# Attention with sinks and a window, then a gated feed-forward: the third group's rows loaded ahead of the output weights, its keys turned by the DMA crossbar

## The chip, the cores and the metric

The kernel runs on one core of a Trainium2 chip. A core has TensorE (PE, matrix products, with PEld for its weight loads), VectorE (DVE), ScalarE (ACT), GpSimd (POOL) and SyncE (SP), which share one SBUF, and 16 DMA engines that serve the queues of SP, ACT and POOL. The metric is the device time of one execution in microseconds. Smaller is better.

## What is computed

The first half is attention over 4 batches, 8 heads, 768 positions and a head size of 64, where a query sees the 4 first positions (the sinks) and the last 128 up to itself. The second half is a gated feed-forward block on the 3072 rows of 512 that come out of it.

```python
def _attn_ref(q, k, v, n_sink, window):
    scores = scale * np.matmul(q, k.transpose(0, 1, 3, 2))
    keep = is_sink | in_window
    scores = np.where(keep, scores, -1000000000.0)
    ...
    a = a / (np.sum(a, axis=-1, keepdims=True) + 1e-09)
    return np.matmul(a, v).astype(np.float32)

def _moe_ref(x, w_gate, w_val, w_out):
    g = x @ w_gate
    silu = g * (1.0 / (1.0 + np.exp(-g)))
    val = x @ w_val
    return (silu * val @ w_out).astype(np.float32)
```

Inputs and output are float32; the kernel computes in bf16 with float32 sums.

## The kernel before

The attention is cut into 12 groups of 256 positions, three to a batch: groups 0 to 2 are batch 0, 3 to 5 batch 1, and so on. The feed-forward is cut into eight blocks of rows (SIZES: three of 256, four of 512, one of 256). Block 3, for one, takes its rows from groups 3 and 4.

A group goes through these steps. Its rows of k and q come in (load_nat, L106: four DMAs of 128 KB on POOL's queue, which cast to bf16; tile nat) and its v (load_v, L143, or load_vm, L120). Keys and queries are turned so that the head dimension lies on partitions, into kT and qT, which hold a batch. There are two ways of turning: step_TN (L273) makes four TensorE transposes for one tensor and one half of 128 positions and has the result copied out of PSUM; xbar (L287) has SP issue a DMA transpose for each half, two to a tensor, and no engine copies anything. Then come the scores and their exponentials (step_S1, L360, step_S2, L408, step_S3, L416: products s with 52 or 18 matrix instructions, six exponentials of 128x512 on ACT, four mask products on DVE; for a group that is not the first of its batch also the sink scores pk and their exponential es, L432 and L438), the products with the values (step_PV, L469: four steps a group, tile o; for groups that are not the first of their batch the first step begins with step_sinks, L447, whose first product reads es), the division by the sum (DVE, tiles rcp and xn) and the turn of the result into xT (step_X, L523: from group 3 on a DMA transpose on SP).

A block of the feed-forward is gates (L611: for each slice the product pg, a tanh on ACT, the product pv, two operations on DVE, into ht) and then downs (L644: for 128 rows twelve products pd with the output weights wo, copied out by ACT and stored; for blocks 0 to 2 the store is issued by ACT, then by SP).

The order is written by hand. `tc.manual_schedule()` is on, so each engine runs its instructions in the order in which the program makes them. TensorE's stream is a list of units (gates and downs), and weave (L714) puts attention steps into numbered units. In the first weave (L860) units 4 to 11 are the gates of blocks 0 and 1 together, 12 to 17 the gates of block 2, and 18 to 23 the downs of blocks 0, 1 and 2, two each. Steps that are put into a downs unit are spread over its twelve products in the order in which they are listed (L645 to L656). A step that SP or DVE has to do after a product is put off until the next flush.

Three things tie the queues together. POOL, ACT and SP each work in order, so an instruction that waits holds back everything behind it on its engine. A DMA waits until the DMA that last used its completion semaphore has landed: POOL has eight of these in rotation, and SP and ACT share eight others. And nat has a single buffer from group 4 on (natp, L64), so that the load of the next group's rows waits until the crossbar has read the group before. Two small POOL instructions are only there to hold back what follows them: behind (L701) waits until the end of a block's xT has landed, turned (L705) until a group's qT has.

Ahead of the weave POOL issues, in this order (L803 to L818): gate weights, rows and values of group 2, gate weights, the four output weights (load_out, L166, 384 KB each), rows and values of group 3, then the clearing of the sinks' tile vcl, whose eight small loads SP issues, and the building of the mask.

## Time and profile before

| | us |
|---|---|
| median of three runs | 233.8 |
| the three runs | 233.5, 233.8, 235.35 |
| the profiled execution | 233.03 |
| its span in the profile | 231.2 |
| PE busy | 226.0 (98% of the span) |
| DVE busy | 151.1 (65%) |
| ACT busy | 106.3 (46%) |
| POOL busy | 84.8 (37%) |

The granted clock of TensorE is full in all 40 slices of the page. Times within the profile count from the start of the span. In a timeline a row has start, length, engine, line, operation, tile written and tile read, shape and count; a bracket at its end is the idle time of that engine just before and what ended it. A row of the chain in order of time has start, length and what ran. Queues are shown as engines with a q (SPq, ACTq); a DMA's row there is the time that its issuing took, not its transfer.

### The profile page before, as it was taken

What the parts mean: (1) busy time and instruction counts of PE and PEld (TensorE: products, weight loads), DVE (VectorE), ACT (ScalarE), POOL (GpSimd) and SP (SyncE); (2) the same over time, 40 slices, a digit from 0 to 9 for tenths busy, and PEclk for the clock granted to TensorE, in tenths of its full rate; (3) what the DMA queues carried; (4) which work ended last, traced back from release to release, by engine and by line L of the source; (5) the groups of instructions that cost most, each with busy time, mean ns of one, the idle gap of its engine ahead of it and who ended that gap; (6) DMA issues with size and microseconds to landing.
All of it is one profiled execution on the core that took longest, in us unless ns stands there. A gap on an engine that the chain in (4) does not pass through costs nothing.

```text
span 231.2 us, 5467 instructions
## 1 busy us (share of the span) xinstructions
PE 226.0 (98%) x2171; PEld 126.8 (55%) x2171; DVE 151.1 (65%) x327; ACT 106.3 (46%) x212; POOL 84.8 (37%) x123
## 2 busy tenths in 40 slices
PE   7989999999999999999999999999999999999994
PEld 3669545786556854455454454454454544487443
DVE  5898888767650797960897960697960599778000
ACT  4784496367523827323626412735512823333221
POOL 8997965960500906904526064362000000000000
PEclk9999999999999999999999999999999999999999
DMA  7999999999998998998999999989814102000132
GB/s 134 164 188 178 179 199 206 163 155 125 154 168 211 80 132 103 145 197 124 134 124 118 147 87 203 144 107 131 94 48 136 48 0 45 3 0 0 69 116 91
DMA packets 112008, 28.04 MB, mean 121 GB/s; under 512 B 99056, under 2 KB 109040, under 8 KB 111984
## 3 DMA queue, kind: packets, MB, share of 16 engines
q0 software_dynamic: 79904, 14.29, 80.7%
q1 hardware_dynamic: 30672, 11.58, 28.5%
q10 hardware_dynamic: 1408, 1.84, 2.8%
q8 instruction: 17, 0.28, 0.5%
q14 instruction: 7, 0.06, 0.1%
HBM read 29.13 MB, written 6.29 MB: 153 GB/s over the span
## 4 chain that ended last, share of the span: by engine, by line
PE 93%; DMA 4%; DVE 1%; ACTq 0%; ACT 0%; issue 0%
PE pg L564 27%; PE pv L564 27%; PE pd L657 27%; PE o L494 3%; PE s L382 3%; DMA wg<-in_moe_w_gate_dram 3%; DMA st<-in_q_dram 2%; PE o L463 1%; PE pn L279 1%; PE o L454 1%; PE pk L432 1%; PE s L326 0%; PE px L543 0%; DVE kT L755 0%; PE pt L746 0%; PE s L765 0%
## 5 line engine op out<-in xcount | busy, mean ns | idle before, releaser
L592 DVE SCALAR_TENSOR_TENSOR u<-th,pg 128x512 bf16<-128x512 f32 x72 | 49.1, 683 | 45.3 <-ACT th L584 44.9
L564 PE MATMUL pg<-xT,wg 128*128 128x512 bf16 (+1 forms) x368 | 74.2, 333 | 0.5 <-DMA wg<-in_moe_w_gate_dram 0.5
L564 PE MATMUL pv<-xT,wv 128*128 128x512 bf16 (+1 forms) x368 | 74.1, 333 | 0.0
L584 ACT ACTIVATE th<-pg 128x512 f32<-128x512 f32 x72 | 43.8, 608 | 59.4 <-PE pg L564 59.2
L657 PE MATMUL pd<-wo,ht 128*128 128x512 bf16 (+2 forms) x300 | 65.9, 370 | 0.0
L564 PEld LDWEIGHTS <-wg 128*128 128x128 bf16 x368 | 35.2, 98 | 26.5 <-DMA wg<-in_moe_w_gate_dram 0.7
L564 PEld LDWEIGHTS <-wv 128*128 128x128 bf16 x368 | 34.6, 98 | 22.8 <-issue 0.2
L607 DVE TENSOR_TENSOR ht<-u,pv 128x512 bf16<-128x512 bf16 x60 | 41.2, 686 | 4.5 <-PE pv L564 0.4
L657 PEld LDWEIGHTS <-ht 128*128 128x128 bf16 x300 | 27.6, 98 | 28.4
L662 ACT ACTIVATE ot<-pd 128x512 f32<-128x512 f32 (+1 forms) x24 | 14.3, 595 | 50.2 <-PE pd L657 50.2
L395 ACT ACTIVATE e<-s 128x512 bf16<-128x512 f32 x54 | 28.5, 614 | 5.8 <-PE s L382 5.4
L113 POOL DMA_DIRECT2D nat<-in_k_dram x20 | 17.8, 896 | 28.6 <-DMA qT<-nat 27.1
L511 DVE TENSOR_TENSOR xn<-o,rcp 128x256 bf16<-128x256 f32 x45 | 17.9, 420 | 0.7
L128 POOL DMA_DIRECT2D vm<-in_v_dram x24 | 17.8, 772 | 1.1 <-DMA va<-in_v_dram 0.8
L113 POOL DMA_DIRECT2D nat<-in_q_dram x20 | 17.8, 908 | 1.0 <-DMA wg<-in_moe_w_gate_dram 0.8
L494 PEld LDWEIGHTS <-e 128*128 128x128 bf16 x256 | 11.5, 98 | 6.0 <-issue 0.2
L404 DVE TENSOR_TENSOR e<-e,maskq 128x768 bf16<-128x768 bf16 x24 | 13.1, 552 | 1.9 <-ACT e L395 1.9
L151 POOL DMA_DIRECT2D va<-in_v_dram x12 | 10.7, 921 | 4.5 <-DMA wo<-in_moe_w_out_dram 2.5
L703 POOL CAST warmed<-xT 1x1 f32<-1x1 bf16 x3 | 0.5, 175 | 28.5 <-DMA xT<-xn 28.5
L503 DVE RECIPROCAL rcp<-o 128x4 f32<-128x4 f32 x48 | 7.1, 171 | 4.8 <-PE o L494 4.5
L664 DVE TENSOR_SCALAR ot<-pd 128x128 f32<-128x128 f32 x1 | 0.3, 292 | 14.3 <-PE pd L657 14.3
L333 ACT ACTIVATE e<-s 128x512 bf16<-128x512 f32 x16 | 8.3, 625 | 0.3 <-PE s L326 0.3
(86 smaller groups left out, 141.4 us busy)
## 6 DMA issues: line engine op xcount, KB each, us to landing
out_dram<-ot SPq DMA_DIRECT2D x17, 256.0 KB
nat<-in_k_dram POOLq DMA_DIRECT2D x20, 128.0 KB, 4.2
nat<-in_q_dram POOLq DMA_DIRECT2D x20, 128.0 KB, 5.2
va<-in_v_dram POOLq DMA_DIRECT2D x12, 128.0 KB, 5.5
wg<-in_moe_w_gate_dram POOLq DMA_DIRECT2D x6, 256.0 KB, 7.1
wv<-in_moe_w_val_dram POOLq DMA_DIRECT2D x6, 256.0 KB, 7.6
wo<-in_moe_w_out_dram POOLq DMA_DIRECT2D x4, 384.0 KB, 11.1
out_dram<-ot ACTq DMA_DIRECT2D x6, 256.0 KB
```

The costliest lines, as they stand in the source:

```text
L113: nc.gpsimd.dma_start(x[:, i, j].rearrange("p (h d) -> p h d", d=D), src[b, :, t0:t0 + P].rearrange("h p d -> p h d"))
L128: nc.gpsimd.dma_start(vms[b][p0:p1, t - 1, :, 0:D], v[b, :, t0:t0 + p1 - p0].rearrange("h p d -> p h d"))
L395: nc.scalar.activation(e_t[g][:, e0:e0 + 512], pss[g][w, i], AF.Exp, scale=scale)
L404: nc.vector.tensor_tensor(e, e, m.broadcast_to([P, 2, 384]), op=ALU.mult)
L494: nc.tensor.matmul(o, l, r, start=(c == 0 and i == 0), stop=(i == len(mms) - 1), skip_group_check=True)
L511: nc.vector.tensor_tensor(xn, po[:, :, 0:D], rcp.broadcast_to([P, 4, D]), op=ALU.mult)
L564: nc.tensor.matmul(ps[:, i * n:(i + 1) * n], ws[fi][:, c, fo * P:(fo + 1) * P], xTs[tb][:, c], start=(c == 0), stop=(c == DMC - 1))
L584: nc.scalar.activation(th, pg, AF.Tanh, scale=0.5)
L592: nc.vector.scalar_tensor_tensor(u, th, 1.0, pg, op0=ALU.add, op1=ALU.mult)
L607: nc.vector.tensor_tensor(hts[tb][:, f:f + 512 // SIZES[tb]].rearrange("p a n -> p (a n)"), u, pv, op=ALU.mult)
L657: nc.tensor.matmul(po, hts[tb][:, f, ts * P:(ts + 1) * P], wos[f // n][:, f % n, lo:hi], start=(f == 0), stop=(f == DFC - 1))
L662: nc.scalar.activation(ot, po, AF.Copy, scale=0.5)
```

## The change

The rows and values of group 3 are loaded ahead of the four output weights, and the clearing of vcl and the sinks' small loads go ahead of both. The keys of group 3 are turned by the crossbar, two DMA transposes that SP issues as soon as the rows are there. In units 14 and 15 only the queries of group 3 are still turned on TensorE: one step of four transposes in each unit, where there were two, both copied out by ACT. Group 3's fourth product with the values moves from unit 20 into unit 19; group 4's scores (step_S1) move from the end of unit 19 into unit 20, ahead of step_S2 and step_S3.

```diff
     load_gate(5)
-    for i in range(4):
-        load_out(i)
-    load_nat(3)
-    load_v(3)
     nc.gpsimd.memset(vcl, 0.0)
     nc.gpsimd.memset(vcl[:, :, D:D + 1], 1.0)
     load_sinks(vcl, 1, B)
+    load_nat(3)
+    xbar(3, (0,))
+    load_v(3)
+    for i in range(4):
+        load_out(i)
     build_maskq()
...
-        ((14, 14, 15, 15), TN(3, "aa")),
+        ((14, 15), [A(step_TN, 3, 1, j, "aa") for j in range(2)]),
         (15, [A(xbar, 4)]), (15, [A(load_nat, 5)]), (19, [A(xbar, 5, (0,))]),
         *one(17, 3), (18, [A(step_ks, 1)]), (18, [A(step_vsb, 1)]),
-        ((19, 19, 19, 20), PVs(3)), (19, [S1(4)]), (20, [L(A(step_S2, 4), A(step_S3, 4))]), (20, Xs(3)), (20, [A(xbar, 5, (1,))]),
+        ((19, 19, 19, 19), PVs(3)), (20, [S1(4), L(A(step_S2, 4), A(step_S3, 4))]), (20, Xs(3)), (20, [A(xbar, 5, (1,))]),
```

## The prediction

> **What bounds the kernel now.** I read the page's busy shares first, then its chain that ended last, then that chain in order of time around the change, then the queues beside it.

> ```profile
> PE 226.0 (98%) x2171; PEld 126.8 (55%) x2171; DVE 151.1 (65%) x327; ACT 106.3 (46%) x212; POOL 84.8 (37%) x123
> ...
> PE 93%; DMA 4%; DVE 1%; ACTq 0%; ACT 0%; issue 0%
> ```

> TensorE (PE) is busy for 98% and is 93% of the chain; the DMA share of it lies before 15 us. So after 15 us a microsecond counts only if PE's own work shrinks, or if PE is made to wait. The chain in order of time (start, length, what) shows the work that is touched:

> ```profile
> 46.41 0.45 PE pn L279 x8
> ...
> 48.60 0.45 PE pn L279 x8
> ...
> 59.52 0.82 PE s L382 x41
> 60.35 0.23 PE pk L432 x8
> 60.58 0.97 PE pd L657 x4
> 61.55 0.24 PE o L494 x8
> 61.79 2.59 PE pd L657 x12
> 64.38 0.22 PE o L454 x4
> ```

> Group 3 is turned in two lots of eight (pn). Group 4's scores (s, pk) stand inside the output projections (pd), and its sink product (o L454) 4.86 us behind their start, without a gap. ScalarE (ACT) between the two:

> ```profile
> 61.39 0.62 ACT L662 ACTIVATE ot<-pd 128x512 f32<-128x512 f32 x1
> 62.04 0.38 ACTq L665 DMA_DIRECT2D out_dram<-ot  x1
> 62.46 1.57 ACT L395 ACTIVATE e<-s 128x512 bf16<-128x512 f32 x3 [0.45 <-ACT ot L662]
> 63.91 0.30 ACT L438 ACTIVATE es<-pk 128x128 bf16<-128x128 f32 x1
> ```

> The sink product needs es, which ends at 64.21, just in time. Last, the loop that feeds groups 4 to 6: SP's crossbar turns, POOL's loads behind them, and the scores of group 6 on PE.

> ```profile
> 49.52 2.58 SPq L293 DMA_TRANSPOSE kT<-nat  x2
> ...
> 61.98 2.74 SPq L293 DMA_TRANSPOSE kT<-nat  x2
> 64.82 3.72 SPq L538 DMA_TRANSPOSE xT<-xn  x2
> 68.63 2.55 SPq L293 DMA_TRANSPOSE qT<-nat  x2
> 71.28 2.56 SPq L538 DMA_TRANSPOSE xT<-xn  x2
> ```

> ```profile
> 57.27 1.75 POOL L113 DMA_DIRECT2D nat<-in_k_dram  x2 [6.22 <-DMA qT<-nat]
> 75.32 0.18 POOL L703 CAST warmed<-xT 1x1 f32<-1x1 bf16 x1 [14.54 <-DMA xT<-xn]
> 88.44 0.17 POOL L709 CAST warmed<-qT 1x1 f32<-1x1 bf16 x1 [7.31 <-DMA qT<-nat]
> ```

> ```profile
> 89.15 0.84 PE L382 MATMUL s<-qT,kT 64*128 64x256 bf16 x18
> ```

> POOL's bracketed waits are landing times: group 4's queries 57.27, group 4's turned result (xT) 75.32, group 6's queries 88.44, only 0.71 us before PE uses them. SP is back to back from 61.98 to 73.84, so whatever delays nat of group 4 runs through this loop undiminished.

> **The change, part by part.** Durations are of the profiled execution: 233.03 us, span 231.2; the median of the runs shown is 233.8, 0.8 higher, and I carry the change over to it.

> *Keys off PE.* Each lot of eight transposes becomes four: 2 x 0.45 / 2 = 0.45 us less on PE, on the path. Two ACT evictions (kT, 0.59 each) go too and are worth nothing: ACT waited 59.2 us for PE in its gate rows alone.

> *Scores of group 4 later.* They move behind four more pd (0.86) and the last product of group 3 (0.24), so 59.52 becomes 59.52 - 0.45 + 1.10 = 60.17; no work is added. But between scores and sink product stood s and pk 1.06, sixteen pd 3.45 and a product 0.24; now stand 1.06 and twelve pd 2.59, so PE is there 3.65 behind S, the scores' start. ACT: the second projection is finished 0.43 before S, its eviction ends at S + 0.21, its store is issued to S + 0.61, six exponentials start from S + 0.66 every 0.48 us (1.57 for three of 0.61 each), es starts at S + 3.54 and ends at S + 3.84; with the 0.10 seen before (64.21 to 64.31) PE loads it at S + 3.94, against S + 3.58 without a wait. That is a new wait of 0.36, bounds 0 (the store issue slips past the exponentials) and 0.7 (the last masks, 0.55 each on DVE, late as well); I take 0.35. PE so far: -0.45 + 0.35 = -0.10.

> *Order of the loads.* The DMA engines are full from 24 to 54 us (slices of 9, 150 to 210 GB/s), so what lands last there depends on the sum of bytes. The four wo loads, landed by about 42.6 (issued up to 29.9, at most 12.7 to landing), now stand behind six loads of 128 KB: at the 153 GB/s of 49 to 51.5 us 0.86 us each, 5.1 in all, plus the turns below: 49.0. First use is 54.29: nothing, with 5 us of cover. POOL's own order costs nothing either: its mask build (41.2 to 42.3) still ends long before group 4's masks at 61, and the copy of the sinks (50.72) may slip some 2 us and is used at 57.58.

> *Two new turns.* SP issues them (1.2 us each) when group 3's keys land, near 36 to 39; SP next has work at 49.52, so nothing queues behind them there. Their price is DMA time ahead of group 4's rows. A turn moves 131 KB. Alone it takes 0.52 (54.5 to 56 us: 250 GB/s). Among loads the trace has two rows. From 51.5 to 54 us 512 packets of 256 B (one turn) and 1,534 of 128 B moved, 131 GB/s in all: the loads got 196 of the 382 KB that 153 GB/s give, 1.21 us lost. From 96.5 to 98.5 us (packets counted likewise) one turn cost the loads 0.64. In the first, packets took up to 1.27 us at 52.4, a stop that the second lacks and that the loop of before thus already holds. So I take 0.65 a turn, 1.3 for both; ends 0 (the lost bytes were not the bound) and 2.4.

> [...]

> *What 1.3 us do.* All landings of the loop shift by it; SP's end of issue to landing is 1.48 (73.84 to 75.32).
> - qT of group 4: 57.27 to 58.6, used at 60.1: hidden.
> - xT of group 3: 68.54 + 1.48 = 70.0 to 71.3, used at 72.5: hidden.
> - qT of group 5: 71.18 + 1.48 = 72.7 to 74.0, used at 74.5: hidden by 0.5.
> - xT of group 4: 75.32 to 76.6, used at 77.5: hidden by 0.9. POOL's wait on it is what holds back group 6's loads (v, then nat), and SP's turns of group 6 wait for those.
> - qT of group 6: 88.44 to 89.74, and PE comes at 89.15 - 0.10 = 89.05: a wait of 0.69.
> Behind it, group 7's scores come at 108, its turns at 95 to 100: slack ends it. ACT's stores find their lanes taken by other turns than before (one store waits for xT of group 3, 71.3 instead of 70.98); ACT's next work is at 72.94.

> Sum: -0.45 + 0.35 + 0.69 = +0.59 us. 233.03 becomes 233.6; on the median, 233.8 becomes 234.4.

> **The rivals.**
> 1. *The cover holds*: the turns cost the loop under 0.7 us. For it: alone 2 x 0.52 is close, and a stop of 1.2 us in before's own loop need not recur. Against: the DMA is full just then. Time: -0.45 + 0.35 = -0.10, 233.7; with es in time as well 233.35. PE-bound as this is, no more than the 0.45 can be gained.
> 2. *The turns stop the loads* (the side I do not forecast: slower by over 1%). One turn among loads lasted from 51.5 to 54; if the loads stood still for all of both, group 4's rows are 5.0 late, qT of group 6 lands at 93.4 and PE waits 4.4 us there: 238.1. It decides from a delay of 3.1 us (2.4 + 0.71). Against: the loads kept half their rate in that row. [...]
> 3. *The output weights are late*: 49.0 would have to become 54.3 for the first. Each microsecond past it is one of PE; for 1% they would need 8 us. The trace has them within 12.7 of issue. I give this little.

> **How the numbers follow.** 1% is about what a measurement of this kernel can tell from no change: 2.3 us. Chances: forecast (a wait of 0.2 to 2.2 us for group 6's queries) 0.55; rival 1 0.26; rival 2 0.15; rival 3 0.02; a gain over 1%, for which no row has the PE time, 0.02. Forecast and rival 1 lie within 1%: 0.81; slower 0.17; faster 0.02. The range goes from rival 1 without the es wait (233.35, less 0.35 for the spread of the runs, 233.5 to 235.35) to the edge of 1%: 233.0 to 236.1. That leaves out rival 2 and what is beyond it. The forecast alone, with delays up to 2.4, is 233.7 to 235.5.

> **What would show it.** Right: two lots of four pn; es ending about 3.8 us behind the first s of group 4, PE's weight load of the sinks waiting for it by some 0.35; POOL's wait for qT of group 6 ending at 89 to 90.5 with PE's scores of group 6 directly behind it; no pd waiting on wo. Wrong: PE's scores of group 6 unmoved with POOL released by 88.9 (rival 1); group 4's or 5's scores waiting for their qT, and loads at a stand during the new turns (rival 2); a pd waiting on a DMA (rival 3).

## The result and the profile after

The changed kernel takes 235.75 us (median of 22 runs, 234.26 to 238.07) against 233.46 us for the kernel before (22 runs on the same chip, 232.53 to 235.46). The ratio is 1.0088, with a 95% interval of 1.0066 to 1.0111: about 2.1 us slower, 0.9%. That is in the range of 233.0 to 236.1, but 1.3 us above the predicted 234.4. Medians here and below are of all runs of a kernel, while the ratios leave out single executions that ran over 1.5% above the fastest of their kernel, so the two can differ.

The profiled execution took 236.93 us, span 235.1. It is a run 1.2 us above its median, so its waits may be on the large side, and its first gate products begin 0.59 us later than in the profile of before (15.68 against 15.09 us), ahead of anything that the change touches. The other profiles without added instructions start there between 14.87 (with four new turns) and 15.77 us (the kernel before with spare turns), so I leave that out. A bracket at a row's end names the wait ahead of it. First the busy shares, the chain's shares by engine and its shares by line, from the page of after:

```profile
PE 223.7 (95%) x2137; PEld 125.9 (54%) x2163; DVE 151.7 (65%) x327; ACT 105.6 (45%) x210; POOL 84.6 (36%) x123
...
PE 78%; DMA 9%; DVE 4%; POOL 2%; issue 2%; ACT 2%; SPq 2%; ACTq 0%; POOLq 0%; DVEq 0%
PE pg L564 23%; PE pv L564 22%; PE pd L657 22%; DMA xT<-xn 4%; PE o L494 3%; PE s L382 3%; DMA rows<-in_q_dram 2%; DMA nat<-in_k_dram 2%; SPq L293 2%; ACT e L395 1%; DMA qT<-nat 1%; DVE ht L607 1%; PE s L326 1%; PE o L463 1%; DVE u L592 1%
```

PE lost three points of its share and 15 of its share of the chain. DMA has 9% of the chain where it had 4%, and the names beside it are those of the loop: xT<-xn, nat<-in_k_dram, qT<-nat, and SP's turns (SPq L293). Where PE now stands still, from its timeline (a row's start and length, then what ran):

```profile
46.78 0.39 PE L279 MATMUL pn<-ident,nat 128*128 128x128 bf16 x4
...
48.75 0.39 PE L279 MATMUL pn<-ident,nat 128*128 128x128 bf16 x4
...
54.22 3.62 PE L657 MATMUL pd<-wo,ht 128*128 128x512 bf16 x15
...
60.65 0.89 PE L382 MATMUL s<-qT,kT 64*64 64x192 bf16 x52
...
64.64 0.29 PE L454 MATMUL o<-vsb,es 32*128 32x260 bf16 x4 [0.17 <-ACT es L438]
...
79.91 1.03 PE L564 MATMUL pg<-xT,wg 128*128 128x256 bf16 x8 [1.66 <-DMA xT<-xn]
...
92.69 0.84 PE L382 MATMUL s<-qT,kT 64*128 64x256 bf16 x18 [1.03 <-DMA qT<-nat]
```

The two lots of transposes are halved, no pd waits for the output weights, and the sink product waits for es. Two larger waits are new: 1.66 us for the turned result of group 4 and 1.03 us for the queries of group 6. From 60 to 98 us PE is idle for 3.29 us, where it was idle for 0.02; the three brackets make 2.86 of it, and the rest lies at least in part where the trace lacks single products (26 more weight loads than products are in the page of after, none more in that of before). ScalarE between group 4's scores and its sinks:

```profile
61.36 3.05 ACT L395 ACTIVATE e<-s 128x512 bf16<-128x512 f32 x6 [0.44 <-PE s L382]
64.24 0.34 ACT L438 ACTIVATE es<-pk 128x128 bf16<-128x128 f32 x1
```

The six exponentials run without a break and es ends at 64.58, 3.93 us behind the scores' start; the prediction had 3.84. The bracket of 0.17 understates the wait for it, because it counts from the modelled end of the last pd. The starts tell more. Before (the first two rows) the twelfth pd starts at 64.00 and the sink product 0.31 later, with no wait; after (the third row, in which the trace lacks one of the twelve products, by the gap ahead of it the first) the last pd starts at 64.09, 3.44 behind the scores as worked out, and the sink product 0.55 later. So the wait costs 0.24 us:

```profile
61.63 2.75 PE L657 MATMUL pd<-wo,ht 128*128 128x512 bf16 x12
64.31 0.29 PE L454 MATMUL o<-vsb,es 32*128 32x260 bf16 x4
...
61.93 2.54 PE L657 MATMUL pd<-wo,ht 128*128 128x512 bf16 x11 [0.16 <-issue]
```

Now the queues, SP's turns first, then POOL's releases:

```profile
36.42 17.55 SPq L293 DMA_TRANSPOSE kT<-nat  x4
54.07 2.52 SPq L293 DMA_TRANSPOSE qT<-nat  x2
64.50 2.84 SPq L293 DMA_TRANSPOSE kT<-nat  x2
67.43 3.18 SPq L538 DMA_TRANSPOSE xT<-xn  x2
70.70 2.82 SPq L293 DMA_TRANSPOSE qT<-nat  x2
73.61 2.86 SPq L538 DMA_TRANSPOSE xT<-xn  x2
```

```profile
49.21 0.69 POOL L128 DMA_DIRECT2D vm<-in_v_dram  x1 [2.76 <-DMA wo<-in_moe_w_out_dram]
50.79 0.68 POOL L128 DMA_DIRECT2D vm<-in_v_dram  x1 [0.88 <-DMA wo<-in_moe_w_out_dram]
...
60.23 1.75 POOL L113 DMA_DIRECT2D nat<-in_k_dram  x2 [7.22 <-issue]
...
79.83 0.48 POOL L703 CAST warmed<-xT 1x1 f32<-1x1 bf16 x1 [16.10 <-DMA xT<-xn]
...
92.68 0.17 POOL L709 CAST warmed<-qT 1x1 f32<-1x1 bf16 x1 [6.84 <-DMA qT<-nat]
```

SP's first row merges the two new turns of group 3 with those of group 4's keys, whose issue ends at 53.97, against 52.10 before; the last wo lands near 50.8. POOL's three releases are 60.23, 79.83 and 92.68, where they were 57.27, 75.32 and 88.44: +2.96, +4.51 and +4.24 us, where the prediction shifted all three by 1.3. The last two come within 0.15 us of the landings. The first does not: its row says issue, not DMA, and by the trace's semaphore records group 4's queries landed at 59.11 (before 56.72), +2.39, while POOL's load began 1.12 us behind that landing (before 0.55). Why POOL took 0.57 longer is not shown. So the mechanism is the predicted one, and the time is in two questions: why two turns put the loop's next load off by 3 us, and why the delay grew on its way.

Where PE lost its time, from the starts of the same rows in the two timelines, the last column less the 0.59 of the later start:

```
PE row                              before   after   lost so far
first gate products                  15.09   15.68      0
first pd                             54.13   54.22     -0.50
sink product of group 4 (es)         64.31   64.64     -0.26
gates with group 3's result          72.75   73.24     -0.10
scores of group 5                    74.58   75.22     +0.05
gates with group 4's result          77.46   79.91     +1.86
scores of group 6                    89.15   92.69     +2.95
```

From there to PE's last product it is 139.08 us in both.

A count from the trace's packet records shows the first. Packets begun in each half microsecond (1,024 bytes are wo, 256 bytes a turn; the second column is the length of a wo packet in ns, its time in the DMA engine):

```
from us   wo    ns   turn
40.0      96    97     1
41.0      75    96    73
42.0      74    96    82
43.0      70    96    74
44.0      82    96    58
45.0      76    96    78
46.0      76    96    78
47.0      72    96    68
48.0      25   413     3     (a stop: one packet took 1.0 us)
```

A turn needs 512 such packets. Alone it moves over 500 of them in half a microsecond (537 in the half from 55.0 of before); among wo it moves 78, so that each of the two lasts 3.3 us, and wo goes on at three quarters. That takes (96 - 76) / 96 x 3.3 = 0.7 us of load time a turn, and then comes a stop of 1.2 us from 47.86, in which hardly a packet moved. This stop is not what makes the delay: the run with 112 pairs below has none among its two new turns, and the last 256-byte packet of its group 4 queries ends at 58.23, against 58.39 here and 56.16 before. Of these 2.1 to 2.2 us the count explains 1.4; where the rest arises is not shown.

### The profile page after: what moved, and what is told of

It is laid out like the page before. It is cut to its first block, busy times and chain, and to the rows that moved or that the text cites. A ratio compares the mean times of both kernels' runs of the same rounds, so it can differ in the third digit from the quotient of the medians.

```text
span 235.1 us, 5428 instructions
## 1 busy us (share of the span) xinstructions
PE 223.7 (95%) x2137; PEld 125.9 (54%) x2163; DVE 151.7 (65%) x327; ACT 105.6 (45%) x210; POOL 84.6 (36%) x123
## 4 chain that ended last, share of the span: by engine, by line
PE 78%; DMA 9%; DVE 4%; POOL 2%; issue 2%; ACT 2%; SPq 2%; ACTq 0%; POOLq 0%; DVEq 0%
PE pg L564 23%; PE pv L564 22%; PE pd L657 22%; DMA xT<-xn 4%; PE o L494 3%; PE s L382 3%; DMA rows<-in_q_dram 2%; DMA nat<-in_k_dram 2%; SPq L293 2%; ACT e L395 1%; DMA qT<-nat 1%; DVE ht L607 1%; PE s L326 1%; PE o L463 1%; DVE u L592 1%
## 5 line engine op out<-in xcount | busy, mean ns | idle before, releaser
L564 PE MATMUL pv<-xT,wv 128*128 128x512 bf16 (+1 forms) x361 | 73.3, 332 | 0.2
L657 PE MATMUL pd<-wo,ht 128*128 128x512 bf16 (+2 forms) x289 | 64.5, 370 | 0.7 <-issue 0.2
L607 DVE TENSOR_TENSOR ht<-u,pv 128x512 bf16<-128x512 bf16 x60 | 41.2, 687 | 4.8 <-PE pv L564 0.4
L657 PEld LDWEIGHTS <-ht 128*128 128x128 bf16 x300 | 27.5, 98 | 28.4
L662 ACT ACTIVATE ot<-pd 128x512 f32<-128x512 f32 (+1 forms) x24 | 14.3, 596 | 53.2 <-PE pd L657 47.5
L395 ACT ACTIVATE e<-s 128x512 bf16<-128x512 f32 x54 | 28.4, 616 | 4.4 <-PE s L382 4.4
L113 POOL DMA_DIRECT2D nat<-in_k_dram x20 | 17.8, 897 | 30.3 <-DMA qT<-nat 22.1
L113 POOL DMA_DIRECT2D nat<-in_q_dram x20 | 17.8, 910 | 0.0
L494 PEld LDWEIGHTS <-e 128*128 128x128 bf16 x256 | 11.6, 98 | 6.1 <-issue 0.2
L703 POOL CAST warmed<-xT 1x1 f32<-1x1 bf16 x3 | 0.8, 277 | 29.0 <-DMA xT<-xn 29.0
L382 PE MATMUL s<-qT,kT 64*64 64x64 bf16 (+4 forms) x366 | 7.9, 218 | 1.1 <-DMA qT<-nat 1.0
```

Of the source, the lines that this page charges most:

```text
L113: nc.gpsimd.dma_start(x[:, i, j].rearrange("p (h d) -> p h d", d=D), src[b, :, t0:t0 + P].rearrange("h p d -> p h d"))
L382: nc.tensor.matmul(pss[g][w, lo // 8][part, 64 * (lo % 8):64 * (lo % 8) + 64 * (hi - lo)], kTs[b][r, p, k0:k0 + kn], qTs[b][r, p, cc:cc + ...
L395: nc.scalar.activation(e_t[g][:, e0:e0 + 512], pss[g][w, i], AF.Exp, scale=scale)
L494: nc.tensor.matmul(o, l, r, start=(c == 0 and i == 0), stop=(i == len(mms) - 1), skip_group_check=True)
L564: nc.tensor.matmul(ps[:, i * n:(i + 1) * n], ws[fi][:, c, fo * P:(fo + 1) * P], xTs[tb][:, c], start=(c == 0), stop=(c == DMC - 1))
L607: nc.vector.tensor_tensor(hts[tb][:, f:f + 512 // SIZES[tb]].rearrange("p a n -> p (a n)"), u, pv, op=ALU.mult)
```

## The experiments

In the first eight runs theory A is that the two turns' DMA time reaches group 4's rows and the loop hands it on. Rival B puts the cost on the order of the loads, C on the later scores, E on the turns' place among the wide wo loads, F on a price that does not depend on how many turns there are. In the last three F, G and H stand for what is written there.

**The order alone.**

```diff
     load_nat(3)
-    xbar(3, (0,))
     load_v(3)
...
-        ((14, 15), [A(step_TN, 3, 1, j, "aa") for j in range(2)]),
+        ((14, 14, 15, 15), TN(3, "aa")),
```

and the scores at their old place.

> The changed order of loads alone: group 3's rows and values ahead of the output weights, but its keys turned on TensorE as before, no new turn, group 4's scores in their old place. Theory A (the two new crossbar turns take DMA time ahead of group 4's rows, and all landings of the loop that feeds groups 4 to 6 shift): without the turns the loop stands as before, result of group 4 landing by 75.0 to 76.0, queries of group 6 by 88.0 to 89.2, time 233.2 to 234.0, ratio to before 0.998 to 1.003. Rival B (the order of loads does it: output weights last in line hold up group 4's rows and POOL's value loads): landings late by 2 to 4 us as in the changed kernel, time 235.0 to 236.0.

Measured: 233.55 against 233.31 us, ratio 1.0003 (0.9975 to 1.0031). POOL's releases are those of before (57.27, 75.32, 88.44) but for tenths:

```profile
57.33 1.75 POOL L113 DMA_DIRECT2D nat<-in_k_dram  x2 [6.93 <-DMA qT<-nat]
...
75.21 0.18 POOL L703 CAST warmed<-xT 1x1 f32<-1x1 bf16 x1 [14.39 <-DMA xT<-xn]
88.84 0.17 POOL L709 CAST warmed<-qT 1x1 f32<-1x1 bf16 x1 [7.81 <-DMA qT<-nat]
```

Group 3's rows ahead of the output weights cost nothing, as predicted. Rival B falls.

**The changed kernel with the scores at their old place.**

```diff
-        ((19, 19, 19, 19), PVs(3)), (20, [S1(4), L(A(step_S2, 4), A(step_S3, 4))]), (20, Xs(3)), ...
+        ((19, 19, 19, 20), PVs(3)), (19, [S1(4)]), (20, [L(A(step_S2, 4), A(step_S3, 4))]), (20, Xs(3)), ...
```

> The changed kernel with group 4's scores and group 3's fourth product put back where they were. Theory A: the loop is as late as in the changed kernel and sets the end, so no gain: group 4's scores wait up to 1.5 us for their queries, the waits on group 4's result and group 6's queries are shorter by the same, time 235.2 to 236.2. Rival C (the move of the scores costs the time, by the late es and what ACT does after it): 233.2 to 234.0.

Measured: 237.42 us, ratio 1.0117 (1.0066 to 1.0167). PE waited for group 4's queries (their landing is 60.79 by the semaphore records; POOL's load began a microsecond later):

```profile
61.91 1.75 POOL L113 DMA_DIRECT2D nat<-in_k_dram  x2 [8.56 <-issue]
...
60.92 0.89 PE L382 MATMUL s<-qT,kT 64*64 64x192 bf16 x52 [1.63 <-DMA qT<-nat]
...
78.83 0.89 PE L382 MATMUL s<-qT,kT 64*64 64x192 bf16 x52 [2.71 <-DMA qT<-nat]
```

The later scores are not the cost, and rival C falls. Nor do they hide much: in the changed kernel the queries land at 59.11, 1.54 us ahead of use, and here PE was ready for them at 59.3 by the bracket. What made PE wait here is a landing 1.7 us later than in the changed kernel, beside a fetch of instructions at 58.56 (see below). The time of 237.42 is above the expected 235.2 to 236.2. The interval overlaps that of the changed kernel, so what the move is worth in time stays open.

**The scores alone**, in the kernel before (the edit above, the other way round).

> The kernel before with the move of group 4's scores and group 3's fourth product alone. Theory A: PE waits 0.2 to 0.45 us for es, the loop is not touched, time 233.6 to 234.0, ratio 1.000 to 1.003. Rival C: 234.8 or more, ratio over 1.006.

Measured: 233.3 us, ratio 1.0012 (0.9993 to 1.0032), with the one new wait:

```profile
64.51 0.29 PE L454 MATMUL o<-vsb,es 32*128 32x260 bf16 x4 [0.17 <-ACT es L438]
```

The predicted wait for es is there: 0.17 in the bracket, 0.24 by the starts as in the changed kernel, against 0.35.

**Two buffers for the rows**, so that group 5's need not wait for the turns of group 4. For the room, the last tiles of the output use a pool of their own.

```diff
-    natp = pool("natp", 1)
+    natp = pool("natp", 2)
...
+    olast = pool("olast", 1)
...
-            ot = opool.tile([P, hi - lo], FP32, ...
+            ot = (olast if last else opool).tile([P, hi - lo], FP32, ...
```

> The changed kernel with two buffers for the rows of groups 4 and on, so that group 5's rows need not wait until group 4's queries are turned (the two output tiles of the last unit get a pool of their own for the space). The turns stay. Theory A, with the loop as the way by which their delay gets to PE: group 4's result lands by 72 to 75 and group 6's queries by 85 to 88.5, no wait there; left are -0.45 for the keys, 0.35 for es and 0 to 1 us for group 4's queries, which are now turned among more loads: 233.2 to 234.4. Rival D (the turns slow PE or the later groups in another way than through this one wait): 235 or more.

Measured: 237.58 us, ratio 1.0124 (1.0075 to 1.0173): a miss. Its profiled execution took 238.34 us, so I read only the place of the wait from it:

```profile
63.83 0.89 PE L383 MATMUL s<-qT,kT 64*64 64x192 bf16 x52 [3.77 <-DMA qT<-nat]
```

The waits at group 4's result and group 6's queries are gone, but group 5's rows, free to load early, now load beside the turns of group 4's queries (their loads are issued from 52.73, the turns from 53.70), and PE waits 3.8 us for those. In this one profile, then, the single buffer was also what kept the loads off the turns.

**One new turn**: only the first half of the keys is turned by the crossbar.

```diff
-    xbar(3, (0,))
+    xbar(3, (0,), (0,))
...
-        ((14, 15), [A(step_TN, 3, 1, j, "aa") for j in range(2)]),
+        ((14, 15, 15), [A(step_TN, 3, *ij, "aa") for ij in ((1, 0), (0, 1), (1, 1))]),
```

> The changed kernel with one new turn instead of two: the first half of group 3's keys by the crossbar, the second half on TensorE (three steps of four transposes instead of two). Theory A (each turn among loads takes 0.8 to 1.2 us of DMA time ahead of group 4's rows, and the loop of turns and loads carries that to the result of group 4 and the queries of group 6): group 4's queries landed by 58.3 to 59.4 (57.3 in the kernel before, 60.2 in the changed one), waits of PE between 0.2 and 1.5 us in all, ratio to before 1.001 to 1.005. Rival F (not the amount counts: any new turn there costs the same, by changed semaphore lanes or SP's order): as the changed kernel, 1.007 to 1.011.

Measured: 234.18 against 233.16 us, ratio 1.0045 (1.0026 to 1.0063). Of the loop's transfers PE waits only for the queries of group 5, 0.58 us by its bracket.

**Four new turns**: the queries of group 3 as well, none on PE (`xbar(3)`, and the line with step_TN removed).

> The changed kernel with four new turns: keys and queries of group 3 both by the crossbar, no transposes of group 3 on TensorE (0.45 us less PE work than in the changed kernel, 0.9 less than before). Theory A: group 4's queries landed by 62 to 64, so that group 4's scores themselves wait 1.5 to 4 us, and the clock may halve behind such a wait; ratio 1.013 to 1.03. Rival F: as the changed kernel, 1.005 to 1.011.

Measured: 239.13 us, ratio 1.0199 (1.0163 to 1.0235). With no new turn 1.0012 (the scores alone), one 1.0045, two 1.0088, four 1.0199: the price goes by the number of turns, 0.3 to 0.5% each with what PE saves already in it. A fixed price (F) falls. Counted from the packet records, the last 256-byte packet of group 4's queries ends at 56.16 us (before), 57.14 (one), 58.39 (two), 59.81 (four): 0.9 to 1.1 us a turn. These are single executions; the profiles without a new turn spread from 55.81 to 56.60. The expected wait at group 4's scores did not come. With four, PE first waits at group 3's own scores and then at group 5's:

```profile
53.27 0.84 PE L382 MATMUL s<-qT,kT 64*128 64x256 bf16 x18 [2.76 <-DMA qT<-nat]
...
78.72 1.50 PE L382 MATMUL s<-qT,kT 64*64 64x192 bf16 x52 [2.12 <-DMA qT<-nat]
```

**The turns alone, for nothing.** The kernel before, with the keys of group 3 turned a second time into a spare tile that nothing reads; its own order of loads, so that the turns fall among packets of 128 bytes, the other loads of groups 3 and 4.

```diff
     load_sinks(vcl, 1, B)
+    spare = const.tile([P, NP2, 256], BF16)
+    for j in range(2):
+        nc.sync.dma_start_transpose(spare[:, :, j * P:(j + 1) * P], nats[3][:, 0, j])
     build_maskq()
```

> The kernel before, in its own order of loads and with group 3 turned on TensorE as before, plus two turns of group 3's keys into a spare tile that nothing reads: the price of two turns by itself, here among the 128-byte loads of groups 3 and 4 rather than among the output weights. Theory A: group 4's queries land 1.6 to 3.5 us later than 57.3, PE waits for group 6's queries or group 4's result, ratio 1.003 to 1.011. Rival E (the price comes from the turns' meeting the output weights, among small packets they are nearly free): landing later by 0.8 us at most, ratio under 1.002.

Measured: 235.48 us, ratio 1.012 (1.0094 to 1.0146), just past the expected 1.011, though no engine computes anything else than before. The profiled execution is 2.0 us above this median:

```profile
60.65 1.75 POOL L113 DMA_DIRECT2D nat<-in_k_dram  x2 [9.17 <-DMA qT<-nat]
...
80.22 0.18 POOL L703 CAST warmed<-xT 1x1 f32<-1x1 bf16 x1 [16.07 <-DMA xT<-xn]
...
93.21 0.17 POOL L709 CAST warmed<-qT 1x1 f32<-1x1 bf16 x1 [7.17 <-DMA qT<-nat]
```

```profile
80.31 1.03 PE L564 MATMUL pg<-xT,wg 128*128 128x256 bf16 x8 [1.00 <-DMA xT<-xn]
...
93.22 0.84 PE L382 MATMUL s<-qT,kT 64*128 64x256 bf16 x18 [1.17 <-DMA qT<-nat]
```

The same three releases of POOL are late by 3.4, 4.9 and 4.8 us, and PE waits at the same two places. This shows theory A by itself: two turns, with nothing gained from them. It also ends rival E, since here no wo packet was near.

**Rows ahead of values** for groups 6 and 5, to take the delay off group 6's queries.

```diff
-A(behind, 3, 511), A(load_v, 5), A(load_nat, 6)]
+A(behind, 3, 511), A(load_nat, 6), A(load_v, 5)]
```

> The changed kernel with group 6's rows loaded ahead of group 5's values, both behind the wait for group 4's result. Theory A: group 6's queries land some 2 us earlier, so PE's wait for them (1.0 us in the profile of the changed kernel) goes and the wait for group 4's result (1.7 us) stays; group 5's values, issued 3.6 us later, still land before their use at 84; ratio 1.003 to 1.007. Rival G (the wait at group 6 only shows a delay that comes back elsewhere, or the values are late): 1.008 or more.

Measured: 242.54 us, ratio 1.0393 (1.0356 to 1.043): a miss. The wait at group 6 went (its queries landed at 89.67), and a larger one came for group 5's values:

```profile
87.79 0.26 PE L463 MATMUL o<-vm,e 64*64 64x65 bf16 x2 [4.26 <-DMA vm<-in_v_dram]
...
88.58 0.60 PE L463 MATMUL o<-vm,e 64*64 64x65 bf16 x29 [0.53 <-DMA vm<-in_v_dram]
```

I had counted group 5's values as having slack, and had not looked up when they are read.

**Why the delay grew.** From SP's end of issue to the landing, the turn of group 4's result took 1.48 us before (73.84 to 75.32) and 3.36 after (76.47 to 79.83). The packet records show that all its data had moved by 77.74; then the DMA engines moved no data for 2.09 us, but for one packet of 16 KB in the queue that the page lists as instruction (q8, 17 packets, 0.28 MB), begun at 77.65, which took 1.1: a fetch of instructions. In the run with the spare turns the gap is 2.56 us, with a fetch at 78.12; in the other profiles that I counted, those of the runs below among them, it is 0.50 to 0.71. (One of these, with one new turn, has a fetch 0.12 us ahead of the landing, without effect.) The trace has 17 such fetches to some 4,300 rows of PE and PEld, one to about 256, which is why I put them down to TensorE; no row names the engine. Rows ahead of values has the same thing at group 4's queries: data done at 58.09, a fetch at 58.03, landing at 60.25. The changed kernel shows that it does not always follow: there the data were done at 58.39, a fetch came at 58.32, and they landed at 59.11. The last three runs move the fetches: small products on a tile of zeros are added to those that keep PE busy in the first 4.3 us, which their results do not outlive.

```diff
-    fill(7, bank([P, 512], FP32, "w"), 512)
+    fw = bank([P, 512], FP32, "w")
+    fill(4, fw, 512)
+    for _ in range(115):
+        nc.tensor.matmul(fw[0:32, 0:16], zero[:, 0:32], zero[:, 0:16], start=True, ...
```

(6 and 17 in place of 4 and 115 in the third. No run leaves the wide products out altogether, so what they do for the clock is not shown.)

> The changed kernel with 112 more pairs of weight load and matrix product on TensorE in the first 4.3 us (small ones, in place of three wide ones that only keep the clock up; their result is never used), so that every 16 KB fetch of instructions comes 112 pairs earlier in the program: by the trace of the changed kernel the one at 77.65 us would come at about 82.6, when no crossbar turn is in flight, and the one at 67.22 at about 68.6. Theory F (a fetch that meets a turn in flight stops it): the last turn of group 4's result lands about 1.5 us earlier, at 77.8 to 78.8 instead of 79.83, PE's wait for it falls from 1.66 to 0.5 at most, the queries of group 6 land at 91.0 to 91.9 instead of 92.68; 1.001 to 1.005 of the kernel before. Rival G (the fetches are beside the point, the landings grow by queueing alone): 79.4 to 80.3, a wait of 1.2 to 2.0, 1.007 to 1.011 as the changed kernel.

> The kernel before with the same 112 small pairs in the first 4.3 us. It prices the pairs themselves: 0.998 to 1.004 by both theories, with the queries of group 4 landing at 57 to 58. By F the fetches then come near 59.7, 67.2 and 76.0, the second among the turns of group 3's result as the one at 65.89 does now, so that the queries of group 6 land at 88 to 89; by G at 88.4 as well.

> The changed kernel with 16 more pairs only, which brings the fetch at 77.65 to about 76.1, when the turns of group 4's result are still being issued (73.61 to 76.47). Theory F: the stop stays, the result lands at 79.2 to 80.4, wait 1.0 to 2.2, 1.006 to 1.011 of the kernel before. Rival H (the small pairs, or any other start, would mend it): as the run with 112 pairs. Rival G: as the changed kernel, 1.007 to 1.011, so that G is told from F by the other run.

Measured: the changed kernel with 112 more pairs 234.7 us, ratio 1.005 (1.0027 to 1.0074); the kernel before with the same 112 pairs 233.89, 1.0013 (0.9994 to 1.0033); the changed kernel with 16 more pairs 236.44, 1.0132 (1.0088 to 1.0177). The changed kernel with 112:

```profile
73.01 2.64 SPq L538 DMA_TRANSPOSE xT<-xn  x2
```

```profile
59.91 1.75 POOL L113 DMA_DIRECT2D nat<-in_k_dram  x2 [7.22 <-issue]
...
78.19 0.18 POOL L703 CAST warmed<-xT 1x1 f32<-1x1 bf16 x1 [14.78 <-DMA xT<-xn]
...
90.66 0.17 POOL L709 CAST warmed<-qT 1x1 f32<-1x1 bf16 x1 [6.66 <-DMA qT<-nat]
```

The fetch came at 79.34 (I had reckoned 82.6), when the turn had landed. POOL's release by the result comes at 78.19, 0.65 us behind the last data, and both waits of PE are gone from its timeline; a start 0.8 us later than in the run with the pairs alone takes part of that back in this one profile. POOL's delay against before hardly grows any more: +2.64 at 59.91, +2.87 at 78.19, +2.22 at 90.66.

The third run's fetches did not come where I had put them: that at 76.1 came at 79.19, 0.13 us behind the landing (79.06, a gap of 0.50). But two others met turns: one at 57.84 was followed by a stop from 58.34 to 59.82, in which hardly a packet moved, and group 4's queries landed at 60.93, 1.8 us later than in the changed kernel:

```profile
61.06 0.89 PE L382 MATMUL s<-qT,kT 64*64 64x192 bf16 x52 [0.54 <-DMA qT<-nat]
```

Over the profiles such pairs recur (a fetch, then a stop, that is a stretch in which hardly a packet moved, from the packet records):

```
kernel              fetch at   stop             turns in flight
before              65.89      66.65 to 68.24   yes
before              85.17      85.78 to 87.2    yes
before              57.48      none             no
before              76.11      none             no
after               46.95      47.86 to 49.03   yes
after               67.22      68.26 to 69.71   yes
after, 16 pairs     57.84      58.34 to 59.82   yes
after, 112 pairs    67.88      68.93 to 70.44   yes
after, 112 pairs    79.34      none             no
```

In the kernel before with 112 pairs a fetch at 88.26 among turns was followed by a stop of only 0.5 us (89.58 to 90.12). A count over all thirteen profiles, from 36 to 170 us, bears the pairs out: 62 fetches began with turns moving (20 or more packets of 256 bytes in the half microsecond before and again after), and 61 were followed within 1.6 us by 0.6 us or more at under 60 GB/s. Of moments with turns moving as much and no fetch near, taken every quarter of a microsecond, 22% were. So G (the fetches beside the point) falls, by this and by the release at 78.19. H (any pairs mend it) falls by the third run. In time it is less sharp: the intervals of 1.0088 and 1.005 overlap a little, so the part of the 2.1 us that hangs on where the fetches fall is about 0.9 us by the ratios (0.0038 x 233.5), with much room on both sides. The loads also slow down without a fetch (before, 52.19 to 53.73, at 107 GB/s where 153 stood from 49 to 51.5, with single packets of up to 1.5 us), so this is not the only cause, and what in the hardware does it stays open.

No version ran faster than the kernel before.

## Why the prediction was right, and where it was wrong

- *Keys off PE*: right. Two lots of four instead of eight; PE's rows gain the 0.45 us (0.50 by the starts at the first pd), and nothing else.
- *Scores of group 4 later*: right. es ended within 0.1 us of the working, PE's last pd started where it was worked out to (3.44 behind the scores), and the wait cost 0.24 us against 0.35.
- *Order of the loads*: right, nothing. The last wo landed at 50.8, not 49.0, which still left 3.4 us of the 5 us of cover.
- *Two new turns*: this is the first step that failed. 0.65 us a turn was taken, between 0.52 alone and 1.21 among loads, because a stop in the row of 1.21 was held to belong to before's own loop. The runs with one, two and four turns give 0.9 to 1.1 by the last data of group 4's queries, so the price lay nearer to that row. The other row among loads, taken as 0.64, comes to 0.76 at the 153 GB/s that the row of 1.21 went by (1,483 packets of 128 bytes in its 2 us). At the landing the delay is 2.39 where 1.3 stood, just the upper end of the step, 2.4. POOL began its next load another 0.57 us later, which no part of the working foresaw; the 57.27 that was called a landing is the start of that load, 0.55 behind the landing at 56.72. Together +2.96. In price a turn came out somewhat above a load: about 1 us, against 0.86 for 128 KB at the 153 GB/s of 49 to 51.5 us.
- *What 1.3 us do*: "All landings of the loop shift by it" failed too. The delay was not just handed on, it grew: +2.96, then +4.51 at group 4's result, of which 1.38 is the longer gap behind its last data. "Hidden by 0.9" therefore became the largest wait of all, 1.66 by its bracket and 1.81 by the starts. Group 3's result and group 5's queries, called hidden too, cost some 0.15 us each. At group 6's queries a wait of 0.69 was forecast; 1.03 was seen (1.09 by the starts), behind a PE that the waits ahead had already pushed back.
- *The rivals*: the cover did not hold, since PE waits at both places. The loads did not stand still during the turns as the second rival had it (wo went on at three quarters), but its threshold fits: the delay at group 6 was 4.24 in the profiled run, above its 3.1, and that execution is indeed over 1% slower, while the ratio is 0.9%. Forecast and this rival are one mechanism, told apart by size alone, and the size came out between them. By the ratio, PE's saved 0.45 us cost some 2.5 us elsewhere (2.1 + 0.45).

The sum with the measured terms of the profiled run, by the starts: -0.50 + 0.24 + 0.16 + 0.15 + 1.81 + 1.09 = +2.95, against 0.59. The later start (0.59) and a tail behind PE's last product of 3.4 us instead of 3.0 make up the rest of the 3.9 by which the two spans differ. That the median still lies in the range owes more to the range, which reached to the edge of 1%, than to this sum: its largest wait stood in it as hidden.

## What to carry to other kernels

Moving work from a full engine to a queue was paid here where that queue's transfers delayed the next load in a loop (+2.96 us), and a loop with little slack handed the delay on to the rounds behind it (+4.51, +4.24): add up the slack at each round, not only at the last. A queue's next instruction is not a landing (here 57.27 against 56.72): check it against the engine that uses the data. Price a transpose by the crossbar among loads by a row where it runs among loads, stops included (here 0.9 to 1.1 us a turn), and not by the time it takes alone (0.52). Before freeing a buffer or reordering a load to cure a late one, look up what the freed transfer will run beside and who reads what it passes: both cures tried here brought a larger wait than they removed, the first of them as read from one profile.

## What the runs showed of the hardware beyond that

A wait of two microseconds cost more than itself in one run. With four turns, after PE's wait of 2.12 us, the table by stretches (length, then each engine's busy time and count; the third column from the end is TensorE's granted clock) shows:

```profile
76.00:78.70 2.70, 0.60 (x6) 0.30 (x4) 1.37 (x2) 0.60 (x1) 0.00 (x0) 1.00 1.03 229
78.70:82.10 3.40, 3.38 (x68) 2.65 (x69) 0.00 (x0) 1.57 (x3) 2.06 (x4) 0.50 0.44 71
82.10:86.00 3.90, 3.90 (x38) 3.45 (x37) 3.02 (x6) 2.88 (x7) 3.71 (x5) 1.00 1.49 94
```

For 3.40 us the clock is 0.50, and the same 52 score products take 1.50 us instead of 0.89. With rows ahead of values the clock is 0.50 over the 6.8 us from 86.8 to 93.6, around the end (87.79) of a wait of 4.26. The length of a wait does not decide alone: in the run with the scores at their old place the 52 products behind a wait of 2.71 us took 0.89 (mean clock over its span 0.998, against 0.993 with four turns). With the waits of the changed kernel itself, 1.66 and 1.03, it is 1.00 from 78 to 84 and from 90 to 97.
